# Three hand-overs between batches and the first tiles of a fused attention and gated-FFN kernel: norms by way of DRAM, folded sums of squares, another order of the G/H tiles

## The chip, the cores and the metric

The kernel runs on one core of a Trainium2 chip. Its time is the device time of that core in microseconds; the kernel before takes 808.06 us (median of three runs, 807.99 to 808.19). All runs that are told here were in the fast state at a granted TensorE clock of 0.997 to 1.000, so no difference between them is one of the clock.

## The reference, cut to what matters

```python
def _attn_ref(q, k, v, tau):                 # q, k, v: (4, 6016, 256) float32
    qn = q / (np.linalg.norm(q, axis=1, keepdims=True) + 1e-06)
    kn = k / (np.linalg.norm(k, axis=1, keepdims=True) + 1e-06)
    s = kn.transpose(0, 2, 1) @ qn / tau     # 256 x 256 for each batch
    a = np.exp(s - s.max(-1, keepdims=True))
    a /= a.sum(-1, keepdims=True) + 1e-09
    return v @ a

def _moe_ref(x, w_gate, w_val, w_out):       # x: 24064 x 256, hidden 1536
    gate = 1.0 / (1.0 + np.exp(-(x @ w_gate)))
    return gate * (x @ w_val) @ w_out
```

Attention here mixes the 256 channels, so it is one 256x256 matrix `a` for each of four batches. The kernel multiplies `a` into the weights (G = a·w_gate, H = a·w_val) and runs the gated feed-forward straight on v.

## The kernel before

A batch is 12 chunks of 512 tokens (the last has 384), a chunk is 12 steps; chunks and steps are counted from 0. One step is a gate product and a value product (two matmuls of 512 columns each), a tanh on ScalarE, a product on VectorE that gives a tile of `hT`, in most steps a sum or difference of `hT` tiles on VectorE (`sums`, here called a sum), and some output matmuls of the chunk before, whose results GpSimd's additions join. Everything for the next batch (scores, norms, exponentials, G and H) is spread over these steps as side work. I call slots 96 and later of a batch, where the next batch's attention is finished, a hand-over; there are three. The parts that the change touches:

```python
    def norms_mm(b):                      # column sums of the squares, on TensorE
        s["n"] = psm.tile([P, 2 * CB], FP32, tag="m", name="ps_n")
        norm_mms(s["n"], s["acc"], TPC, True, True)          # 2*4*2 = 16 matmuls of one column

    def spread_both(b):                   # k's inverse norms to a row, the same in all partitions
        s["rk_ps"] = psm.tile([P, C], FP32, tag="m", name="ps_rk")
        for i in range(CB):
            mm(s["rk_ps"][:, ds(i * P, P)],
               s["r"][:, CB + i : CB + i + 1].to_broadcast([P, P]), ident_f, True, True)
    # copy_rk: ScalarE copies rk_ps to rk_sb

    def scale_x(b, j):                    # VectorE: scores x q's norms x k's norms
        nc.vector.scalar_tensor_tensor(out=s["x"][:, j, :], in0=s["s"][:, j, :],
            scalar=s["r"][:, j : j + 1], in1=s["rk_sb"], op0=ALU.mult, op1=ALU.mult)

    def sums_start(b, ni, pl, tag):       # starts the row sums with the small constant
        ps_r = pl.tile([P, ni, 2], FP32, tag=tag, name="ps_r")
        mm(ps_r, ones_row, eps_row[:, :ni, :], start=True, stop=False, skip_group_check=True)
    # ... cut ...
        s0 = 8 * FC + 2                   # = slot 98, in side_work
        at(s0, norms_mm, n)
        at(s0 + 1, root_seed, n)          # square root: seed on VectorE, 13 steps on GpSimd
        at(s0 + 1, root_steps, n)
        at(s0 + 10, norms_inv, n)
        at(s0 + 12, spread_both, n)
        at(s0 + 13, copy_rk, n)
        at(s0 + 14, scale_x, n, 0)        # and n, 1; then exps, all_sums, gh_tiles, gh pieces
    # ... cut ...
    gh_slots = ((5, 6, 7), (8,), (9, 10), (11,), (12,), (13, 14), (15,))   # batch 0: G/H pieces by step
    # for f, the step of chunk 0 of batch 0:
    #     glu(..., between = piece 4 in step 0);  ...;  for i in gh_slots[f]: gh(0, gh_first[i], pso, "o")
```

The chunk that comes next needs v turned: `transpose_v` issues a DMA transpose on SyncE's queue at step 2 of each chunk. The loads are issued on GpSimd's queue.

## Time and profile before

| what | value | how to read it |
|---|---|---|
| time | 808.06 us | median of three runs |
| span of the profiled run | 806.4 us | first to last instruction |
| start of the span to the first matmul | 6.91 us | varies from 6.49 to 7.00 over all kernels told here, with no order in it |
| first matmul to the first gate matmul of chunk 2, batch 0 | 63.34 us | first loads, batch 0's attention, first G/H tiles |
| from there to the start of the last matmul | 732.87 us | the three hand-overs lie here |
| start of the last matmul to the end | 3.28 us | last copies and stores |

The last four rows come from the trace's starts and add up to the span. I use them because a whole time mixes all four, and two of them move from kernel to kernel without having been touched. The lines of the profile before are in the prediction.

### The profile page before, as it was taken

The numbers are of one execution on the slowest core, as the hardware profiler recorded it, in microseconds if no ns is written. First come the engines' busy times: TensorE is split into PE (matmuls) and PEld (weight loads), VectorE is DVE, ScalarE is ACT, GpSimd is POOL, SyncE is SP. The second block draws the span as 40 slices with busy tenths as digits, with TensorE's granted clock in tenths as the row PEclk, the third lists the DMA queues.
The fourth block names the chain that finished last, engine by engine and source line by source line (L and its number), as shares of the span: only waits on it lengthen the run. The fifth ranks groups of instructions, "written<-read, shape, count | busy, mean of one in ns | idle before, by whom it ended". The sixth has DMA issues, their size and how long they took to land.

```text
span 806.4 us, 17923 instructions
## 1 busy us (share of the span) xinstructions
PE 786.3 (98%) x6786; PEld 501.5 (62%) x6786; DVE 704.4 (87%) x1201; ACT 525.6 (65%) x890; POOL 356.9 (44%) x568
## 2 busy tenths in 40 slices
PE   3899999999999999999999999999999999999998
PEld 2546666666666666666666666666666666666666
DVE  5767999998878999999887999999988898898896
ACT  3666777766667776775666767776666665665664
POOL 4572545444452444335443544433534244434433
PEclk9999999999999999999999999999999999999999
DMA  9995757532567567422367377523422332332402
GB/s 214 204 214 105 125 91 135 103 67 47 102 123 128 90 103 145 87 53 58 83 117 132 72 145 112 105 54 89 64 53 54 87 65 63 84 65 68 85 28 74
DMA packets 78919, 78.50 MB, mean 97 GB/s; under 512 B 51824, under 2 KB 56688, under 8 KB 78832
## 3 DMA queue, kind: packets, MB, share of 16 engines
q0 software_dynamic: 22192, 39.59, 29.4%
q1 hardware_dynamic: 56064, 36.91, 20.6%
q8 instruction: 53, 0.87, 0.4%
q10 hardware_dynamic: 576, 0.85, 0.3%
q14 instruction: 34, 0.28, 0.1%
HBM read 78.64 MB, written 24.64 MB: 128 GB/s over the span
## 4 chain that ended last, share of the span: by engine, by line
PE 94%; DMA 3%; DVE 1%; issue 1%; POOL 0%; ACT 0%; POOLq 0%; DVEq 0%; ACTq 0%
PE ps_val L127 30%; PE ps_gate L127 30%; PE ps_o L127 27%; PE ps_s L127 4%; DMA k_sb<-in_k_dram 3%; PE ps_gh L127 3%; DVE hT L514 0%; PE ps_r L127 0%; PE ps_n L127 0%; DVE acc L284 0%; DVE sums L536 0%; PE ps_rk L127 0%; POOL q_sb L137 0%; PE ps_end L127 0%; ACT g_sb L513 0%
## 5 line engine op out<-in xcount | busy, mean ns | idle before, releaser
L513 ACT ACTIVATE g_sb<-ps_gate 128x512 f32<-128x512 f32 (+1 forms) x576 | 338.2, 588 | 225.5 <-PE ps_gate L127 218.9
L514 DVE SCALAR_TENSOR_TENSOR hT<-g_sb,ps_val 128x512 bf16<-128x512 f32 (+1 forms) x576 | 384.6, 670 | 84.3 <-ACT g_sb L513 74.6
L127 PE MATMUL ps_val<-vT,gh_H 128*128 128x512 bf16 (+1 forms) x1152 | 337.7, 375 | 0.9 <-DVE gh_H L461 0.6
L127 PE MATMUL ps_gate<-vT,gh_G 128*128 128x512 bf16 (+1 forms) x1152 | 337.6, 375 | 0.0
L536 DVE TENSOR_TENSOR sums<-hT 128x768 bf16<-128x768 bf16 (+1 forms) x460 | 275.9, 600 | 0.0
L127 PEld LDWEIGHTS <-sums 128*128 128x128 bf16 x2670 | 183.0, 98 | 82.1
L127 PEld LDWEIGHTS <-gh_H 128*128 128x128 bf16 x1152 | 112.7, 98 | 132.3 <-DVE gh_H L461 1.4
L607 POOL TENSOR_TENSOR out_sb<-out_sb,m_sb 128x256 f32<-128x256 f32 x89 | 78.7, 884 | 239.6 <-ACT out_sb L597 211.1
L127 PE MATMUL ps_o<-w_sums,sums 128*128 128x128 bf16 x1602 | 154.4, 219 | 0.0
L127 PEld LDWEIGHTS <-hT 128*128 128x128 bf16 x1200 | 88.3, 98 | 46.8
L591 POOL TENSOR_TENSOR m_sb<-m_sb 128x128 f32<-128x128 f32 x89 | 42.2, 474 | 159.8 <-ACT m_sb L590 159.8
L127 PEld LDWEIGHTS <-gh_G 128*128 128x128 bf16 x1152 | 97.0, 98 | 14.9 <-DVE gh_G L461 0.3
L127 PE MATMUL ps_o<-w_out_sb,sums 128*128 128x128 bf16 x1068 | 96.2, 219 | 0.0
L127 PE MATMUL ps_o<-w_sums,hT 128*128 128x128 bf16 x1068 | 95.5, 219 | 0.0
L127 PE MATMUL ps_s<-k_sb,q_sb 128*128 128x256 bf16 x376 | 69.2, 286 | 15.4 <-DMA k_sb<-in_k_dram 8.5
L608 POOL TENSOR_TENSOR out_sb<-out_sb 128x256 f32<-128x256 f32 x89 | 77.0, 865 | 7.0
L597 ACT COPY out_sb<-ps_o 128x512 f32<-128x512 f32 x89 | 52.1, 586 | 12.0 <-PE ps_o L127 9.2
L284 DVE TENSOR_TENSOR acc<-acc,sq 128x1024 bf16<-128x1024 bf16 (+1 forms) x66 | 59.8, 905 | 0.0
L592 POOL TENSOR_TENSOR m_sb<-m_sb 128x128 f32<-128x128 f32 x89 | 53.8, 604 | 7.0
L246 ACT ACTIVATE sq<-k_sb 128x1024 bf16<-128x1024 bf16 (+2 forms) x44 | 44.8, 1027 | 12.0 <-DMA k_sb<-in_k_dram 11.8
L127 PEld LDWEIGHTS <-q_sb 128*128 128x128 bf16 x376 | 32.9, 102 | 20.8 <-issue 10.3
L590 ACT COPY m_sb<-ps_o 128x384 f32<-128x384 f32 x89 | 42.6, 478 | 3.4 <-PE ps_o L127 0.6
(83 smaller groups left out, 309.4 us busy)
## 6 DMA issues: line engine op xcount, KB each, us to landing
out_dram<-out_sb SPq DMA_DIRECT2D x43, 512.0 KB, 3.4
v_sb<-in_v_dram POOLq DMA_DIRECT2D x44, 256.0 KB, 5.3
q_sb<-in_q_dram POOLq DMA_DIRECT2D x35, 256.0 KB, 4.6
k_sb<-in_k_dram POOLq DMA_DIRECT2D x35, 256.0 KB, 6.1
q_sb<-in_q_dram POOLq DMA_DIRECT2D x4, 512.0 KB, 11.6
k_sb<-in_k_dram POOLq DMA_DIRECT2D x4, 512.0 KB, 13.5
w_f<-in_moe_w_out_dram POOLq DMA_DIRECT2D x3, 512.0 KB, 9.2
out_dram<-out_sb SPq DMA_DIRECT2D x3, 384.0 KB, 2.8
```

The costliest lines, as they stand in the source:

```text
L127: nc.tensor.matmul(out, lhsT=lhsT, rhs=rhs, start=start, stop=stop, **kw)
L246: nc.scalar.activation(out=sq[:, :nt, :], in_=src[:, :nt, :], func=ACT.Square)
L284: nc.vector.tensor_tensor(out=acc[:, :nt, :], in0=acc[:, :nt, :], in1=st[b]["sq", w][:, :nt, :], op=ALU.add)
L513: nc.scalar.activation(out=g_sb[:, :n], in_=ps_gate[:, :n], func=ACT.Tanh, scale=0.5)
L514: nc.vector.scalar_tensor_tensor(out=hts[b, ci][:, f, :n], in0=g_sb[:, :n], scalar=1.0, in1=ps_val[:, :n], op0=ALU.add, op1=ALU.mult,)
L536: nc.vector.tensor_tensor(out=sums[b, ci, g][:, m, :, : half * P], in0=hT[:, f0 + k0 : f1 : 2, ds(r0 * half * P, half * P)], in1=hT[:, f0 ...
L590: nc.scalar.copy(m, states[p]["ps"][:, : 3 * P].rearrange("p (n c) -> p n c", c=P))
L591: nc.gpsimd.tensor_tensor(out=m[:, 1, :], in0=m[:, 1, :], in1=m[:, 2, :], op=ALU.add)
L592: nc.gpsimd.tensor_tensor(out=m[:, 2, :], in0=m[:, 1, :], in1=m[:, 0, :], op=ALU.add)
L597: nc.scalar.copy(o[:, p : p + half + 1 : half, :], states[p]["ps"].rearrange("p (t c) -> p t c", c=C),)
L607: add(out=ends, in0=ends, in1=states[p]["m"][:, 1:3, :], op=ALU.add)
L608: add(out=ends, in0=ends, in1=mids, op=ALU.subtract)
```

## The change

The intent is to take work off TensorE, which is busy for nearly the whole span: fold the four quarters of the sums of squares on VectorE, so that 4 matmuls remain of 16; replace the two fp32 matmuls that spread k's norms by a VectorE transpose in 32x32 blocks, two DMA writes to a row in DRAM and one read that spreads it; start the row sums in bf16; and in batch 0 put the G/H pieces elsewhere among the gate and value products, on more PSUM banks (PSUM is the memory that matmuls write to; a bank is one buffer of it).

```diff
-    ones_row = consts.tile([1, P], FP32)
+    ones_row = consts.tile([1, P], BF16)
-    eps_row = consts.tile([1, CB, 2], FP32)
+    eps_row = consts.tile([1, CB, 2], BF16)
+    r_wide = consts.tile([P, 32], FP32)
...
+    def acc_fold(b, w):
+        acc = st[b]["acc"][w]
+        for n in (2, 1):
+            nc.vector.tensor_tensor(out=acc[:, :n, :], in0=acc[:, :n, :], in1=acc[:, n : 2 * n, :], op=ALU.add)
...
-        norm_mms(s["n"], s["acc"], TPC, True, True)
+        norm_mms(s["n"], s["acc"], 1, True, True)
...  spread_both: the two matmuls (and copy_rk) go, in their place:
+        nc.vector.transpose(out=rT, in_=r_wide)
+        row = dpool.tile([C], FP32, tag="row", name="row")
         for i in range(CB):
+            nc.sync.dma_start(
+                out=row[ds(i * P, P)].rearrange("(s j) -> s j", j=32), in_=rT[CB + i : P : 32, :]
+            )
+        nc.sync.dma_start(out=s["rk_sb"], in_=row.rearrange("(o c) -> o c", o=1).to_broadcast([P, C]))
...  slots of a hand-over
-        at(s0, norms_mm, n)
+        at(s0 if b == 0 else s0 - 2, acc_fold, n, 0)
+        at(s0 + 1 if b == 0 else s0, acc_fold, n, 1)
+        at(s0 + 3, norms_mm, n)
...
-        at(s0 + 14, scale_x, n, 0)
+        at(s0 + 19, scale_x, n, 0)
...  batch 0's G/H pieces
-    gh_slots = ((5, 6, 7), (8,), (9, 10), (11,), (12,), (13, 14), (15,))
+    gh_mid = {0: 4, 1: 6, 2: 9, 3: 11}
+    gh_end = {0: (5,), 1: (7, 8), 2: (10,), 3: (12,), 4: (13,), 5: (14,), 6: (15,)}
+    gh_banks = ((pso, "o"), (psm, "m"), (pso, "o"), (pss, "s"))
```

Left out: in a hand-over the square root starts three slots later and the spread two slots earlier; the later batches' G/H pieces come two steps apart, and those that no longer fit run in the next batch's first steps.

More of the change, by code (lines that the diff above doesn't have):

```diff
@@ L117 @@
     opool = pool("opool", 2)
+    dpool = pool("dpool", 1, space=bass.MemoryType.DRAM)
     psg = pool("psg", 2, space=PSUM)
@@ L173 @@
     nc.vector.memset(one_two[:, 1:2], 2.0)
-    ones_row = consts.tile([1, P], FP32)
+    ones_row = consts.tile([1, P], BF16)
     nc.vector.memset(ones_row, 1.0)
-    eps_row = consts.tile([1, CB, 2], FP32)
+    eps_row = consts.tile([1, CB, 2], BF16)
     nc.vector.memset(eps_row[:, :, 0:1], 1e-9)
     nc.vector.memset(eps_row[:, :, 1:2], 2e-9)
+    r_wide = consts.tile([P, 32], FP32)
+    nc.vector.memset(r_wide, 0.0)
     shift = consts.tile([P, 1], FP32)
@@ L307, in spread_both @@
         s = st[b]
-        s["rk_ps"] = psm.tile([P, C], FP32, tag="m", name="ps_rk")
+        rT = attp.tile([P, 32], FP32, tag="rT", name="rT")
+        nc.vector.transpose(out=rT, in_=r_wide)
+        row = dpool.tile([C], FP32, tag="row", name="row")
         for i in range(CB):
-            mm(
-                s["rk_ps"][:, ds(i * P, P)],
-                s["r"][:, CB + i : CB + i + 1].to_broadcast([P, P]),
-                ident_f,
-                True,
-                True,
-            )
-    def copy_rk(b):
-        s = st[b]
+            nc.sync.dma_start(
+                out=row[ds(i * P, P)].rearrange("(s j) -> s j", j=32), in_=rT[CB + i : P : 32, :]
+            )
         s["rk_sb"] = attp.tile([P, C], FP32, tag="rk", name="rk_sb")
-        nc.scalar.copy(s["rk_sb"], s["rk_ps"])
+        nc.sync.dma_start(out=s["rk_sb"], in_=row.rearrange("(o c) -> o c", o=1).to_broadcast([P, C]))
     def norms_sqrt(b):
@@ L347, in root_steps @@
         t = attp.tile([P, 2 * CB], FP32, tag="tn", name="t_n")
-        s["r"] = attp.tile([P, 2 * CB], FP32, tag="r", name="r")
+        s["r"] = r_wide[:, : 2 * CB]
         for _ in range(3):
@@ L741 @@
     gh(0, gh_first[3], pso, "o")
+    spill = {}
     def side_work(b):
@@ L784, in side_work, with gh_piece @@
         s0 = 8 * FC + 2
-        at(s0, norms_mm, n)
-        at(s0 + 1, root_seed, n)
-        at(s0 + 1, root_steps, n)
-        at(s0 + 10, norms_inv, n)
-        at(s0 + 12, spread_both, n)
-        at(s0 + 13, copy_rk, n)
-        at(s0 + 14, scale_x, n, 0)
-        at(s0 + 14, scale_x, n, 1)
-        at(s0 + 15, exps, n, 0)
-        at(s0 + 16, exps, n, 1)
-        at(s0 + 18, all_sums, n)
-        at(s0 + 18, gh_tiles, n)
-        for i, piece in enumerate(gh_order):
-            at(s0 + 19 + 9 * i // 4, gh, n, piece, *((pss, "s"), (psm, "m"))[i % 2])
-        return side
-    gh_slots = ((5, 6, 7), (8,), (9, 10), (11,), (12,), (13, 14), (15,))
+        at(s0 if b == 0 else s0 - 2, acc_fold, n, 0)
+        at(s0 + 1 if b == 0 else s0, acc_fold, n, 1)
+        at(s0 + 3, norms_mm, n)
+        at(s0 + 4, root_seed, n)
+        at(s0 + 4, root_steps, n)
+        at(s0 + 10, norms_inv, n)
+        at(s0 + 10, spread_both, n)
+        at(s0 + 19, scale_x, n, 0)
+        at(s0 + 19, scale_x, n, 1)
+        at(s0 + 20, exps, n, 0)
+        at(s0 + 21, exps, n, 1)
+        at(s0 + 23, all_sums, n)
+        at(s0 + 23, gh_tiles, n)
+        for i, piece in enumerate(gh_order):
+            slot = s0 + 24 + 2 * i
+            if slot < NCH * FC:
+                at(slot, gh, n, piece, *((pss, "s"), (psm, "m"))[i % 2])
+            else:
+                spill.setdefault((n, *divmod(slot - NCH * FC, FC)), []).append((gh, (n, piece, psm, "m")))
+        return side
+    gh_mid = {0: 4, 1: 6, 2: 9, 3: 11}
+    gh_end = {0: (5,), 1: (7, 8), 2: (10,), 3: (12,), 4: (13,), 5: (14,), 6: (15,)}
+    gh_banks = ((pso, "o"), (psm, "m"), (pso, "o"), (pss, "s"))
+    def gh_piece(n):
+        gh(0, gh_first[n], *gh_banks[n % 4])
     prev = None
@@ L809 @@
             for f in range(FC):
-                first = (b, ci, f) == (0, 0, 0)
-                glu(b, ci, f, (lambda: gh(0, gh_first[4], pso, "o")) if first else None)
+                mid = gh_mid.get(f) if (b, ci) == (0, 0) else None
+                glu(b, ci, f, None if mid is None else (lambda: gh_piece(mid)))
                 if prev is not None:
@@ L819 @@
                     a_sum(b, ci, 0, OWN_SLOTS[f])
-                for fn, a in side.get((ci, f), ()):
+                for fn, a in spill.get((b, ci, f), []) + side.get((ci, f), []):
                     fn(*a)
-                if (b, ci) == (0, 0) and f < len(gh_slots):
-                    for i in gh_slots[f]:
-                        gh(0, gh_first[i], pso, "o")
+                if (b, ci) == (0, 0):
+                    for i in gh_end.get(f, ()):
+                        gh_piece(i)
             prev = (b, ci)
```

## The prediction

> **What bounds the kernel now.** I read the busy shares first, then the chain that ended last, then TensorE's waits, then TensorE's groups by shape, and last the timeline around the places that the change touches. The first fence has the busy shares and the chain's shares by engine, both from the page.
>
> ```profile
> PE 786.3 (98%) x6786; PEld 501.5 (62%) x6786; DVE 704.4 (87%) x1201; ACT 525.6 (65%) x890; POOL 356.9 (44%) x568
> ...
> PE 94%; DMA 3%; DVE 1%; issue 1%; POOL 0%; ACT 0%; POOLq 0%; DVEq 0%; ACTq 0%
> ```
>
> TensorE's own matmuls are 94% of the chain. The view of TensorE's waits says how much of the rest of its time is a wait for somebody (in total us, times, longest us):
>
> ```profile
> PE ps_s L127 <- DMA k_sb<-in_k_dram: 8.5, 6, 3.1
> PE ps_s L127 <- ACT k_sb L183: 6.9, 1, 6.9
> PE ps_val L127 <- DVE gh_H L461: 0.6, 1, 0.6
> PE ps_gh L127 <- ACT gh_H L459: 0.6, 1, 0.6
> PE ps_val L127 <- DVE hT L514: 0.3, 1, 0.3
> ```
>
> The first two are the first loads, which the change doesn't touch. After them TensorE waits under 2 us in 770. So work leaves the time only if it leaves TensorE, and shows there one for one; VectorE at 87% may not be pushed past TensorE's pace. From one matmul's start to the next I read 216 ns at 512 columns, 56 ns at 128 and 25 ns at 1 or 2. The groups that the change removes or thins are these (busy us, mean ns, idle before):
>
> ```profile
> L127 PE MATMUL ps_rk<-ident_f,r 128*128 128x128 f32 x16 | 2.7, 291 | 0.0
> ...
> L127 PE MATMUL ps_n<-ones_bf,acc 128*128 128x1 bf16 x64 | 2.2, 163 | 0.0
> ...
> L127 PE MATMUL ps_r<-eps_row,ones_row 1*128 1x4 f32 x6 | 1.1, 258 | 0.0
> ```
>
> Their durations overlap, so I don't use the means but the starts in the timeline of the first hand-over (batch 0 to 1):
>
> ```profile
> 173.84 0.54 PE L127 MATMUL ps_n<-ones_bf,acc 128*128 128x1 bf16 x16
> 174.24 0.59 PE L127 MATMUL ps_gate<-vT,gh_G 128*128 128x512 bf16 x2
> ...
> 189.29 0.66 PE L127 MATMUL ps_rk<-ident_f,r 128*128 128x128 f32 x4
> 189.79 0.59 PE L127 MATMUL ps_gate<-vT,gh_G 128*128 128x512 bf16 x2
> ...
> 197.15 0.33 PE L127 MATMUL ps_o<-w_out_sb,sums 128*128 128x128 bf16 x3
> 197.41 0.38 PE L127 MATMUL ps_r<-eps_row,ones_row 1*128 1x4 f32 x2
> 197.72 0.25 PE L127 MATMUL ps_r<-one_two,e_sb 128*128 128x2 bf16 x4
> ```
>
> Each sits between ordinary matmuls, without idle time of its own: TensorE pays all of it.
>
> **What the Trainium skill says.** "TensorE: Matmul & The Clock Gate", section "Wait — 56ns, not 53.3ns?", gives 55 to 56 ns from start to start at 128 columns and a floor of about 25 ns however small the matmul; the trace agrees (56 and 25). "FP8 and Floating Point Precision", section "TensorE Precision Notes", says that true FP32 takes four passes. Here each fp32 matmul leaves two records, 111 ns apart for 128 columns, so 222 ns or four times 56: it agrees in time, not in the count of records. "VectorE: DVE Perf Modes", section "The three transpose paths", says that VectorE's transpose turns 32×32 blocks only, 311 ns for a 128×128 bf16 tile. That is why four norms per partition come out as rows of 32 in separate partitions and must go through DRAM to be joined; no such operation is in this trace. "DMA: Bandwidth & Descriptors", section "Anatomy of one DMA — SWDGE (gpsimd) path", gives about 2 us of fixed cost per DMA. In this trace the smallest stores on the other queues (64 KB) land after 1.5 to 1.6 us, 128 KB ones after 2.0.
>
> **The change, part by part.** Three hand-overs (into batches 1, 2, 3) are changed alike.
>
> *Sums of squares folded.* VectorE adds the four quarters of each accumulator (512 then 256 columns), so 4 matmuls remain of 16. Sixteen took 174.24 − 173.84 = 0.40 us, 25 ns each; twelve are 0.30 us. VectorE pays two additions per accumulator: in the first phase a 128x512 bf16 product took 424 ns and a 128x256 one 292 ns, so about 0.7 us each pair, 1.4 us per hand-over, less a little overlap.
>
> *Spread of k's norms.* The two fp32 matmuls took 189.79 − 189.29 = 0.50 us; all of it goes. ScalarE loses a copy of 0.38 us, which was not on the path. VectorE gains one transpose of 128x32; estimated from the page's 311 ns for four times the columns, 0.1 to 0.3 us.
>
> *Row sums' first matmul in bf16.* The last of the three output matmuls would end its turn at 197.15 + 3 × 0.056 = 197.32, the next useful matmul starts at 197.72: 0.40 us, of which a bf16 matmul of 4 columns needs 0.025. It saves 0.37. In batch 0 the same matmuls end before TensorE has to wait for the exponentials anyway (idle 0.17 us), so nothing is saved there.
>
> Together 0.30 + 0.50 + 0.37 = 1.17 us per hand-over, 3.5 us for three.
>
> *G/H tiles in batch 0.* From 36.8 to 49.0 us TensorE alternates these pieces with the first gate/value matmuls, all pieces through one pair of PSUM buffers. Comparing starts with the 216 ns and 109 ns turns, I find six gaps: 0.13, 0.08, 0.72, 0.08, 0.80, 0.07 us, in sum 1.88. The large two:
>
> ```profile
> 39.22 0.38 PE L127 MATMUL ps_gh<-w_val,e_sb 128*128 128x256 bf16 x2 [0.56 <-ACT gh_H L459]
> ...
> 45.27 0.39 PE L127 MATMUL ps_val<-vT,gh_H 128*128 128x512 bf16 x1 [0.64 <-DVE gh_H L461]
> ```
>
> One is a piece that waits for its buffer, the other a value matmul that waits for VectorE to write the H tile finished just before. The change uses four banks and puts pieces between gate and value, so that a tile is finished earlier. I walked the new order by hand with turns of 0.43 us (two 512-column matmuls), ScalarE at 0.69 and 0.60 us, VectorE at 0.74 and 0.69. The 0.13 stays (nothing before it changed); one wait of about 0.2 appears where the value matmul of step 2 needs the H piece that VectorE writes at 40.7 to 41.1; the rest fits, the last H tile of the second group being written some 0.5 us early. The last piece ends at 47.4 instead of 49.0: 1.55 us saved.
>
> *G/H tiles of the later batches* start five steps later, two steps apart, and one spills into the next batch. TensorE's work is the same and the tile it fills is first used eight steps after: 0.
>
> *New small stalls.* In the first hand-over the second fold falls in a step that has a sum too, and pushes the next gate-value product from 177.2 to about 177.5, near the moment at which TensorE wants its buffer. I allow 0.2 us for all of these.
>
> Sum: 808.06 − 3.5 − 1.55 + 0.2 = 803.2.
>
> **The rivals.**
>
> *The DRAM detour comes late.* VectorE is in order: if the row isn't back at its multiplication, it blocks, both value buffers fill, and TensorE stops. From the norms' step (VectorE at 187.5) to the multiplication there are nine steps of 1.255 us, 11.3 us. Two writes and one read at 2 to 3.5 us each, the read behind the writes, make 4 to 6 us. Against it: 5 us to spare, and the transpose of v behind it on the same issuing engine is needed only at the next chunk, some 10 us on. If it came 2 us late each time, up to 1 us each would be lost after buffering, some 3 us: 806.
>
> *The square root's slots shrink.* It starts three steps later and the inverse stays, so nine steps become six, 7.5 us. GpSimd's chain ran from 177.37 to 182.01, 4.64 us; its seed now comes from VectorE at about 180.8, which ends it at 185.5, and VectorE wants it at 187.4. GpSimd's other additions were moved ahead of it in the order, so they end before. About 1.9 us to spare; if it failed, 0.5 to 1 us per hand-over: 805 to 806.
>
> *VectorE becomes the bound.* Per step it has 0.61 + 0.55 = 1.16 us against TensorE's 1.255. It recovers only 0.1 us per step where each has a sum, so 1.6 us of folds and transpose could lag for many steps. Against it: three of four kinds of fold lie in steps without a sum (0 and 2 of a chunk). It would cost 0.5 us per hand-over: 804.7.
>
> *The start gains less,* because ScalarE or VectorE, served in another order, make TensorE wait elsewhere: half of 1.55 would leave 804.
>
> *Something hidden anyway* (no gain at all) I hold for unlikely, since TensorE has no idle time at these places.
>
> **Range and chances.** All rivals but the first are small and add to the same side, so the range is wider above: 802.4 to 804.8. Even the whole sum without a loss is 0.65%, so over 2% in either direction is next to excluded: 0.01 each. Runs of the kernel before spread by only 0.2 us.
>
> **What would show it.** TensorE's groups: the fp32 row sums gone, 4 records of the spread left of 16, 28 of the folded matmuls left of 64; the waits for gh_H gone from its waits. Starts in the hand-over: 0.10 us for what is left of the norms' matmuls, no gap at the spread, some 0.03 us for the first row-sum matmul. The last piece of batch 0 about 10.7 us after the first gate matmul, instead of 12.3. The row lands within 6 us of the transpose. I am wrong if TensorE's waits list VectorE's multiplication, its fold or the norms in the hand-overs, or if VectorE waits for GpSimd or the DMA there.

## The result

The changed kernel took 806.44 us (median of six runs, 806.03 to 806.69) against 808.11 us for the kernel before. The ratio is 0.9979, 95% interval 0.9966 to 0.9992. A ratio here is the mean time of one kernel's fast runs over that of the other's of the same rounds, so it isn't quite the ratio of the medians. The gain is 1.67 us where 4.9 was predicted, and the time lies outside the range, above it. The outputs are right.

Busy shares and the chain's shares by engine, from the page of the changed kernel:

```profile
PE 783.2 (97%) x6733; PEld 497.8 (62%) x6733; DVE 711.0 (88%) x1217; ACT 524.8 (65%) x887; POOL 356.5 (44%) x568
...
PE 91%; DMA 5%; DVE 2%; POOL 1%; issue 1%; ACT 0%; POOLq 0%
```

TensorE has 53 records fewer and 3.1 us less busy time, so the work did leave it. But its share of the chain fell from 94% to 91%, and the DMA's rose from 3% to 5%: something else now holds it up. TensorE's waits (total us, times, longest us), without the first loads, name it:

```profile
...
PE ps_gate L128 <- DMA vT<-v_sb: 1.0, 1, 1.0
PE ps_r L128 <- ACT e_sb L397: 0.6, 1, 0.6
PE ps_val L128 <- DVE hT L518: 0.3, 1, 0.3
```

The two waits for the H tiles are gone, as predicted, and a new one of 1.0 us for a transposed v stands in their place. The view of TensorE's groups by shape (busy us, mean ns, idle before) has the counts that were predicted, 28 and 4 and no fp32 row sum:

```profile
L128 PE MATMUL ps_n<-ones_bf,acc 128*128 128x1 bf16 x28 | 1.3, 164 | 0.0
L128 PE MATMUL ps_rk<-ident_f,r 128*128 128x128 f32 x4 | 0.7, 300 | 0.0
...
L128 PE MATMUL ps_r<-eps_row,ones_row 1*128 1x4 bf16 x3 | 0.5, 173 | 0.0
```

The places where time went are in TensorE's timeline (start us, duration us):

```profile
51.20 0.59 PE L128 MATMUL ps_val<-vT,gh_H 128*128 128x512 bf16 x2
52.76 0.61 PE L128 MATMUL ps_gate<-vT,gh_G 128*128 128x512 bf16 x2 [0.97 <-DMA vT<-v_sb]
...
177.03 0.24 PE L128 MATMUL ps_n<-ones_bf,acc 128*128 128x1 bf16 x4
177.13 0.59 PE L128 MATMUL ps_gate<-vT,gh_G 128*128 128x512 bf16 x2
...
199.70 0.59 PE L128 MATMUL ps_gate<-vT,gh_G 128*128 128x512 bf16 x2
200.35 0.59 PE L128 MATMUL ps_val<-vT,gh_H 128*128 128x512 bf16 x2
...
202.17 0.55 PE L128 MATMUL ps_o<-w_sums,hT 128*128 128x128 bf16 x7
202.66 0.17 PE L128 MATMUL ps_r<-eps_row,ones_row 1*128 1x4 bf16 x1
202.76 0.25 PE L128 MATMUL ps_r<-one_two,e_sb 128*128 128x2 bf16 x4
```

The first two of these lines belong to chunk 1's first gate product. In the kernel before they were:

```profile
52.91 0.59 PE L127 MATMUL ps_val<-vT,gh_H 128*128 128x512 bf16 x2
53.34 0.59 PE L127 MATMUL ps_gate<-vT,gh_G 128*128 128x512 bf16 x2
```

Four things are to be seen, in this order. (1) At chunk 1's first gate product the turn that should take 0.43 us takes 52.76 − 51.20 = 1.56: 1.13 lost to the transpose of v. The kernel before started the same product without a wait. (2) The norms' matmuls take 0.10 us now, 0.30 less, as predicted. (3) Between the gate and value products at 199.70 there are 0.65 us, not 0.43: a gap of 0.21 that no wait lists. The waits view counts only time in which no matmul's modelled duration runs, and these durations (0.59 for a turn of 0.43) cover the gap. A second gap, 0.14 us, lies at the output matmuls at 201.06. All three hand-overs have both, within 11 ns of each other. (4) The seven output matmuls from 202.17 would end their turn at 202.17 + 7 × 0.056 = 202.56; the next useful matmul starts at 202.76. The bf16 row-sum start therefore takes 0.20 us, not 0.025: some 95 ns before it, its own 25, and 80 after it.

By the four stretches of the trace:

| stretch | before | after | difference |
|---|---|---|---|
| to the first matmul | 6.91 | 6.57 | −0.34 |
| to the first gate matmul of chunk 2 | 63.34 | 63.11 | −0.23 |
| to the start of the last matmul | 732.87 | 730.91 | −1.96 |
| to the end | 3.28 | 3.66 | +0.38 |

The hand-overs gave 1.96 of the predicted 3.3 (3.5 less 0.2), the start 0.23 of 1.55, and the end lost 0.38, which nobody had looked for. (The profiled run was the fastest of the six, 806.03; the others are up to 0.66 slower, and their traces weren't kept. So the four differences add up to 2.15, more than the 1.67 between the medians.)

VectorE's timeline around the multiplication `scale_x` shows what surrounds the gap at 199.9:

```profile
197.20 0.69 DVE L518 SCALAR_TENSOR_TENSOR hT<-g_sb,ps_val 128x512 bf16<-128x512 f32 x1
197.81 1.10 DVE L540 TENSOR_TENSOR sums<-hT 128x768 bf16<-128x768 bf16 x1
198.84 0.86 DVE L305 SCALAR_TENSOR_TENSOR x_sb<-ps_s,r_wide,rk_sb 128x256 f32<-128x256 f32 x2
199.62 0.67 DVE L518 SCALAR_TENSOR_TENSOR hT<-g_sb,ps_val 128x512 bf16<-128x512 f32 x1
```

The multiplication (0.86 us) follows a sum that took 1.10 instead of its usual 0.55, so the next `hT` product, which frees the value bank, starts 2.4 us after the last one (197.20 to 199.62) where a step is 1.255. TensorE has two such banks and runs out of them. The row of norms wasn't late: the next fence has SyncE's queue (issue start, time to issue) and, from the view of the tile `rk_sb`, the landing time of the read.

```profile
187.44 1.18 SPq L321 DMA_DIRECT2D row<-rT  x2
189.70 0.33 SPq L325 DMA_DIRECT2D rk_sb<-row  x1
```

```profile
DMA to landing us min/median/max: 3.3/3.5/3.7
```

The writes went out at 187.44, the read at 189.70, and 3.5 us later the row was there: about 193.2, 5.6 us ahead of the multiplication at 198.84.

### The profile page after: what moved, and what is told of

Its sections match the earlier page's. It is cut to its first block, busy times and chain, and to the rows that moved or that the text cites. A ratio compares the mean times of both kernels' runs of the same rounds, so it can differ in the third digit from the quotient of the medians.

```text
span 804.3 us, 17846 instructions
## 1 busy us (share of the span) xinstructions
PE 783.2 (97%) x6733; PEld 497.8 (62%) x6733; DVE 711.0 (88%) x1217; ACT 524.8 (65%) x887; POOL 356.5 (44%) x568
## 4 chain that ended last, share of the span: by engine, by line
PE 91%; DMA 5%; DVE 2%; POOL 1%; issue 1%; ACT 0%; POOLq 0%
PE ps_val L128 29%; PE ps_gate L128 29%; PE ps_o L128 27%; PE ps_s L128 4%; DMA k_sb<-in_k_dram 3%; PE ps_gh L128 2%; DMA vT<-v_sb 1%; DMA v_sb<-in_v_dram 1%; DVE hT L518 1%; DVE sums L540 0%; DVE x_sb L305 0%; POOL w_gate L197 0%; POOL w_val L197 0%; ACT g_sb L517 0%; DVE acc L287 0%
## 5 line engine op out<-in xcount | busy, mean ns | idle before, releaser
L540 DVE TENSOR_TENSOR sums<-hT 128x768 bf16<-128x768 bf16 (+1 forms) x460 | 279.9, 609 | 0.0
```

The lines of the kernel that those rows point to most:

```text
L540: nc.vector.tensor_tensor(out=sums[b, ci, g][:, m, :, : half * P], in0=hT[:, f0 + k0 : f1 : 2, ds(r0 * half * P, half * P)], in1=hT[:, f0 ...
```

## The experiments

Theories of the missing 3.2 us were set against each other in four places. For the start: the transpose of v is late because of what the DMA engines have ahead of it, or because its v was loaded too late. For the hand-overs: VectorE is held by the folds, by the DMA detour, or by the place at which the multiplication now falls. For the row sums: the cost is of a matmul with one row, or of the row sums as such. For the end: the DRAM tile delays it. Each kernel below was timed in rounds with the kernel before on the same chip; all give right results. "Third stretch" is the third row of the table above, and it is the sharper measure, since the whole times of kernels with the change spread by 0.3 to 0.9 us. It comes from one profile of each kernel; where an edit leaves the hand-overs alone it repeats within 0.03 us (732.86 to 732.87, and 730.89 to 730.91).

### The new order in batch 0 alone

Edit: the kernel before, with only this part of the change.

```diff
-    gh_slots = ((5, 6, 7), (8,), (9, 10), (11,), (12,), (13, 14), (15,))
+    gh_mid = {0: 4, 1: 6, 2: 9, 3: 11}
+    gh_end = {0: (5,), 1: (7, 8), 2: (10,), 3: (12,), 4: (13,), 5: (14,), 6: (15,)}
+    gh_banks = ((pso, "o"), (psm, "m"), (pso, "o"), (pss, "s"))
```

> The kernel before with only the new order of batch 0's G/H pieces. Theory A (the start is bound by the DMA transpose of the second chunk of v): TensorE's gaps for gh_H go, step 11 of chunk 0 comes about 1.5 us earlier, but TensorE then waits about 1.1 us for vT at the first gate of chunk 1, so the time falls by only 0.3 to 0.6 us. Rival (the prediction's: the gain is real, and the 3.3 us were lost in the hand-overs): the time falls by 1.3 to 1.6 us and no wait for vT shows.

Measured: 807.82 us (807.73 to 807.97) against 808.12, ratio 0.9996 (0.9988 to 1.0005). From the first gate product to that of step 11, chunk 0 is 1.54 us shorter than before (14.17 us against 15.71), so the order itself does what it was meant to. Then TensorE waits 1.0 us for the transposed v. The third stretch is 732.86, unchanged. So the order alone gains some 0.3 us (the interval reaches 1, but the stretch from the first matmul to chunk 2 is also 0.25 us shorter), and the rest of its 1.55 goes into that wait.

### The v of chunk 1 loaded earlier

Edit to the changed kernel: the load of chunk 1's v goes ahead of the last third of the weights.

```diff
     for f0, nf in pieces:
+        if f0 == FG * (NFG - 1):
+            load_v(0, 1)
...
-    load_v(0, 1)
```

> The changed kernel with the load of v's second chunk issued ahead of the last third of the gate and value weights instead of behind it. Theory A: vT lands some 2 to 3 us earlier, the wait of 1.0 us at the first gate of chunk 1 goes, and the time falls by 0.8 to 1.2 us to about 805.4; other waits unchanged. Rival (the DMA queues are full anyway, and whatever is issued first the transpose lands when the bytes before it are through): the wait stays within 0.3 us of what it is, or moves to the G/H pieces that need the last weights, and the time stays at 806.4.

Measured: 806.54 us (806.02 to 806.96) against 808.12, ratio 0.9980 (0.9974 to 0.9987), the same as the change. SyncE could issue the transpose at 40.73 instead of 43.27, but TensorE got it no earlier. (The trace has no landing for this transpose in kernels with the DRAM detour; TensorE's start shows the end of the wait.) TensorE's timeline:

```profile
53.08 0.61 PE L128 MATMUL ps_gate<-vT,gh_G 128*128 128x512 bf16 x2 [1.24 <-DMA vT<-v_sb]
```

The wait is still there, and ends at 53.08 instead of 52.76. So it isn't the issue that is late; the transpose, issued 2.5 us sooner, took at least that much longer.

### Loads that aren't urgent moved behind the transpose

Edit to the changed kernel: v of chunk 2 and the first q and k of batch 1, three loads of 256 KB (bf16) issued between 38.5 and 41.7 us, go behind the copies of w_out on GpSimd, to 49 us and later.

```diff
-            if lb < B:
+            if lb < B and (b, ci) != (0, 0):
                 at(ci * FC + 0, load_v, lb, lci)
...
                     at(8, copy_w_out, i)
+                at(8, load_qk, 1, *groups[0])
+                at(8, load_v, lb, lci)
...
-                at(max(0, s0 - 12), load_qk, n, t0, nt)
+                if g:
+                    at(max(0, s0 - 12), load_qk, n, t0, nt)
```

> The changed kernel with three loads that nobody needs before chunk 1 (v's third chunk and the first q and k group of batch 1, 0.75 MB) issued after GpSimd's casts of the output weights, at 48.7 us instead of 38.5 to 41.2. Theory A2 (the transpose of v's second chunk lands when the backlog on the 16 DMA engines is through, whenever it is itself issued: issued 2.5 us earlier in the run with the early load, it landed no earlier): the backlog ends some 3 us earlier, vT lands before 51.7, the wait of 1.0 us at the first gate of chunk 1 goes and the time falls by 0.8 to 1.2 us, if the first scores of batch 1 don't wait for their loads. Rival (the transpose itself needs its 10 us here): the wait stays within 0.3 us. A third outcome, a new wait of TensorE for q and k of batch 1 at about 55 us in place of the old one, would leave the time at 806.4.

Measured: 805.21 us (805.04 to 805.55) against 808.16, ratio 0.9964 (0.9950 to 0.9977). The same two lines of TensorE's timeline as at chunk 1 of the changed kernel:

```profile
51.34 0.59 PE L128 MATMUL ps_val<-vT,gh_H 128*128 128x512 bf16 x2
51.78 0.59 PE L128 MATMUL ps_gate<-vT,gh_G 128*128 128x512 bf16 x2
```

The turn is 0.44 us, the wait is gone, and the stretch from the first matmul to chunk 2 is 61.78 us, 1.56 less than before. No new wait came for it. In the windows view the mean DMA share from 48 to 54 us is 0.71, where the changed kernel has 1.26 (the view adds up the packets' times, which overlap, so it can pass 1). With the run before, this settles the start: what delays the transpose is the bulk loads that the DMA engines still have to carry. The Trainium skill, "DMA: Bandwidth & Descriptors", section "Queues, rings and completion order", says that each DMA engine goes round between the queue rows it has work for, packet by packet; that would make a transpose share its engines with all open loads. These two runs agree with it, but none shows the packets' order.

### Row sums started with 128 rows

Edit to the changed kernel: the constant is divided by 128 and summed over 128 partitions, with ones in 128 rows as weights, in place of one row.

```diff
-    eps_row = consts.tile([1, CB, 2], BF16)
-    nc.vector.memset(eps_row[:, :, 0:1], 1e-9)
-    nc.vector.memset(eps_row[:, :, 1:2], 2e-9)
+    eps_row = consts.tile([P, CB, 2], BF16)
+    nc.vector.memset(eps_row[:, :, 0:1], 1e-9 / P)
+    nc.vector.memset(eps_row[:, :, 1:2], 2e-9 / P)
...
-        mm(ps_r, ones_row, eps_row[:, :ni, :], start=True, stop=False, skip_group_check=True)
+        mm(ps_r, ones_bf, eps_row[:, :ni, :], start=True, stop=False, skip_group_check=True)
```

> The changed kernel with the constant of the row sums made by a matmul over 128 rows (weights of ones, constants divided by 128) instead of one row. Theory B (the switch to a one-row weight and back costs 0.175 us at each hand-over, as the starts show 95 and 80 ns too much): from the last output matmul before to the first row-sum matmul it is one turn of 56 ns and one of 25, the time falls by 0.5 us. Rival (a small matmul after a wide one costs this whatever its rows): the 95 and 80 ns stay, the time is unchanged.

Measured: 805.83 us (805.60 to 805.98) against 808.12, ratio 0.9972 (0.9961 to 0.9982). TensorE's timeline at the first hand-over:

```profile
202.29 0.55 PE L128 MATMUL ps_o<-w_sums,hT 128*128 128x128 bf16 x7
202.68 0.17 PE L128 MATMUL ps_r<-eps_row,ones_bf 128*128 128x4 bf16 x1
202.71 0.24 PE L128 MATMUL ps_r<-one_two,e_sb 128*128 128x2 bf16 x4
```

The start of the row sums comes 0.39 us after the seven (7 × 0.056), and the next 0.03 after it: it now costs the 25 ns that I had predicted for the one-row form. The third stretch fell by 0.58, 0.19 in each hand-over. So the 95 and 80 ns belong to a matmul of one row. Whether to its weights or to its moving operand isn't separated, since both have one row there and 128 here.

### Row sums in fp32 again

Edit to the changed kernel:

```diff
-    ones_row = consts.tile([1, P], BF16)
+    ones_row = consts.tile([1, P], FP32)
-    eps_row = consts.tile([1, CB, 2], BF16)
+    eps_row = consts.tile([1, CB, 2], FP32)
```

> The changed kernel with the row sums' constants in fp32 again. The starts say 0.405 us for the fp32 pair and 0.20 us for the one bf16 matmul: the time rises by 0.6 us for three hand-overs. If the prediction's 0.37 us per hand-over were right, it would rise by 1.1 us.

Measured: 806.84 us (806.62 to 807.45) against 808.09, ratio 0.9986 (0.9979 to 0.9992); the third stretch rose by 0.60, 0.20 for each hand-over. So the step from fp32 to bf16 is worth 0.20, not the predicted 0.37.

### No folds

Edit to the changed kernel: the 16 matmuls back, `norms_mm` still at slot 101.

```diff
-        norm_mms(s["n"], s["acc"], 1, True, True)
+        norm_mms(s["n"], s["acc"], TPC, True, True)
...
-        at(s0 if b == 0 else s0 - 2, acc_fold, n, 0)
-        at(s0 + 1 if b == 0 else s0, acc_fold, n, 1)
```

> The changed kernel without the folding of the sums of squares: 16 matmuls again at each hand-over, VectorE's four additions gone. By the arithmetic on record the folding is worth 12 x 25 ns = 0.30 us per hand-over: the time rises by 0.9 us if VectorE's additions are free. If the additions delay VectorE up to the multiplication (rival D), the gaps at the multiplication go with them, and the time rises by less than 0.3 us or falls.

Measured: 807.52 us (807.08 to 807.80) against 808.09, ratio 0.9993 (0.9985 to 1.0001). The third stretch rose by 0.89, 0.30 in each hand-over: the fold is worth what was predicted. The gaps at the multiplication stay (0.21 and 0.14 us at the first hand-over), so the folds don't make them.

### The spread on TensorE again

Edit to the changed kernel: the two fp32 matmuls and ScalarE's copy back, at slots 110 and 111; the multiplication stays at 117.

```diff
-        nc.vector.transpose(out=rT, in_=r_wide)
-        row = dpool.tile([C], FP32, tag="row", name="row")
...  the three DMAs go
+            mm(s["rk_ps"][:, ds(i * P, P)], s["r"][:, CB + i : CB + i + 1].to_broadcast([P, P]), ident_f, True, True)
...
-        at(s0 + 10, spread_both, n)
+        at(s0 + 12, spread_both, n)
+        at(s0 + 13, copy_rk, n)
```

> The changed kernel with the spread on TensorE again (two fp32 matmuls and ScalarE's copy, at the old steps), the multiplication left at step 117. By the arithmetic on record the spread is worth 0.50 us per hand-over: the time rises by 1.5 us, and the gaps at the multiplication stay (0.3 to 0.4 us per hand-over), because they come of its place and not of the DMA. Rival (the DMA detour itself, its row late or its traffic, makes the gaps): they go, and the time rises by only 0.4 us.

Measured: 807.36 us (807.20 to 807.50) against 808.09, ratio 0.9991 (0.9983 to 0.9999). The third stretch rose by 1.48, 0.49 in each hand-over, as predicted for the two matmuls. The gaps stay (0.21 and 0.14), so the detour doesn't make them either. The whole time rose by only 0.92; 0.38 of the difference to 1.48 is the end of the trace, which is back at 3.28 us, and the rest lies in the start and in the spread of runs.

### The multiplication three steps earlier, and three later

Edits to the changed kernel. The first moves only the multiplication, to slot 114:

```diff
-        at(s0 + 19, scale_x, n, 0)
-        at(s0 + 19, scale_x, n, 1)
+        at(s0 + 16, scale_x, n, 0)
+        at(s0 + 16, scale_x, n, 1)
```

> The changed kernel with the multiplication by the spread norms three steps earlier (step 114, not 117), some 1.4 us after the row lands by the profile; all else in place. Theory C (at step 117 it falls behind a sum that GpSimd's additions stretch to 1.10 us, and its 0.78 us then make the next products late): the 0.21 and 0.14 us gaps on TensorE at each hand-over go or shrink to under 0.1 us in sum, the time falls by 0.7 to 1.0 us. Rival D (VectorE is simply at its bound there by the folds and the transpose): the gaps only move a step or two, the time stays within 0.2 us.

Measured: 805.31 us (804.90 to 805.39) against 808.12, ratio 0.9964 (0.9952 to 0.9977). Both gaps are gone in all three hand-overs, and the third stretch fell by 1.06, 0.35 each (0.21 and 0.14). VectorE's timeline at the new place:

```profile
194.34 0.55 DVE L540 TENSOR_TENSOR sums<-hT 128x768 bf16<-128x768 bf16 x1
194.81 0.87 DVE L305 SCALAR_TENSOR_TENSOR x_sb<-ps_s,r_wide,rk_sb 128x256 f32<-128x256 f32 x2
```

The multiplication takes as long as before (0.87 against 0.86), but the sum ahead of it takes 0.55 instead of 1.10. The row, which lands at about 193.2, is still there in time.

The second moves the multiplication and all that follows it by three steps, to slot 120:

```diff
-        at(s0 + 19, scale_x, n, 0)
+        at(s0 + 22, scale_x, n, 0)
...  exps, all_sums, gh_tiles likewise
-            slot = s0 + 24 + 2 * i
+            slot = s0 + 27 + 2 * i
```

> The changed kernel with the multiplication by the spread norms, the exponentials, the row sums and the G/H pieces all three steps later, so that the multiplication falls in step 120, which has no sum on VectorE. Theory C: the gaps of 0.21 and 0.14 us on TensorE go at all three hand-overs, no new one comes, the time falls by 0.8 to 1.1 us. Rival D (VectorE at its bound): gaps of the same sum some steps later, the time stays within 0.2 us.

Measured: 805.08 us (804.92 to 805.39) against 808.09, ratio 0.9963 (0.9951 to 0.9976). The gaps are gone here too, and the third stretch fell by 1.22. Of this, 1.06 are the gaps again; the other 0.16 lies in the steps of the G/H pieces, which this edit moves as well, and wasn't looked into. So it is the place, not the operation: the same multiplication costs TensorE 0.35 us at 117 and nothing at 114 or 120. Nor is it the long sum alone, since that is still there in this kernel, with an `hT` product behind it and no gap on TensorE:

```profile
197.96 1.10 DVE L540 TENSOR_TENSOR sums<-hT 128x768 bf16<-128x768 bf16 x1
198.99 0.68 DVE L518 SCALAR_TENSOR_TENSOR hT<-g_sb,ps_val 128x512 bf16<-128x512 f32 x1
```

At 114 the multiplication follows a sum of 0.55 us and does no harm, at 120 the sum of 1.10 has no multiplication behind it and does none; in these runs only both together cost TensorE its 0.35.

What makes that sum long is read from the traces; no run of its own tests it. GpSimd's timeline in the changed kernel has this addition:

```profile
197.77 0.73 POOL L612 TENSOR_TENSOR out_sb<-out_sb 128x256 f32<-128x256 f32 x1
```

It starts 0.04 us before the sum that took 1.10, and so it does in all three hand-overs. The whole trace of the changed kernel has 430 sums of this shape. The 200 without a two-input operation of GpSimd beside them take 0.54 to 0.55 us. Of the 75 that start before the GpSimd operation, all but one take this long too. In 127 the GpSimd operation had started first and had more than 0.15 us to go: 122 of these sums end 0.41 to 0.42 us after it does (five aren't stretched), and all 22 sums over 0.86 us are among them. The Trainium skill, "SBUF — State Buffer", section "SBUF: two separate sides", says that VectorE and GpSimd share one pair of ports as an exclusive lock, which a VectorE operation with two SBUF inputs needs against a GpSimd operation that reads SBUF: whoever starts first keeps it. The trace agrees: the sum that comes second waits for the end of the addition, and then needs another 0.41 us of its 0.55. No run took the addition away.

### The parts together

Edit to the changed kernel: slot 120 and the 128-row constant, as above.

```diff
-        at(s0 + 19, scale_x, n, 0)
+        at(s0 + 22, scale_x, n, 0)
...
-        mm(ps_r, ones_row, eps_row[:, :ni, :], start=True, stop=False, skip_group_check=True)
+        mm(ps_r, ones_bf, eps_row[:, :ni, :], start=True, stop=False, skip_group_check=True)
```

> The changed kernel with the multiplication at step 120 and the row sums' constant over 128 rows together. If the two costs are separate, their gains add: 806.44 - 1.36 - 0.61, about 804.5, and only the wait for vT is left of what this study found. If they overlap (both hide behind the same VectorE lag) it is 805.0.

Measured: 804.70 us (804.42 to 805.03) against 808.16, ratio 0.9957 (0.9944 to 0.9969). The third stretch fell by 1.79, just the sum of the two alone (1.22 + 0.58). The wait for v at chunk 1 was 1.4 us.

With the later loads as well:

```diff
                     at(8, copy_w_out, i)
+                at(8, load_qk, 1, *groups[0])
+                at(8, load_v, lb, lci)
```

> The same two with the three later loads as well. If theory A2 holds: a further 0.8 to 1.2 us, about 803.5, which is the time predicted for the change. If not, 804.5 as without them.

Measured: 803.47 us (803.26 to 803.61) against 808.16, ratio 0.9941 (0.9929 to 0.9954), span 801.5. It beats both kernels. TensorE's waits, without the first loads:

```profile
...
PE ps_r L128 <- ACT e_sb L397: 0.7, 1, 0.7
PE ps_val L128 <- DVE hT L518: 0.3, 1, 0.3
```

The wait for the transposed v is gone; what is left belongs to batch 0's exponentials and one `hT` product. That this time lies near the predicted 803.2 vouches for nothing: it takes three repairs to get there.

### A DRAM row that nobody uses

Edit: the kernel before, with a tile in DRAM written and read in each hand-over, for nothing.

```diff
         nc.scalar.copy(s["rk_sb"], s["rk_ps"])
+        row = dpool.tile([P, 2 * CB], FP32, tag="row", name="row")
+        nc.sync.dma_start(out=row, in_=s["r"])
+        unused = attp.tile([P, 2 * CB], FP32, tag="unused", name="unused")
+        nc.sync.dma_start(out=unused, in_=row)
```

> The kernel before, with the norms also written to a small DRAM tile and read back into a tile that nobody uses, once per hand-over; nothing waits for it. The traces so far show from the last matmul to the span's end 3.28, 3.29 and 3.28 us in the three kernels that spread on TensorE, and 3.62 to 4.05 us in the nine that have the DRAM row. Theory E (a DRAM tile in the program, or its place beside the output, makes the last store land later): the tail is 3.6 us or more and the time rises by 0.3 to 0.8 us, with TensorE's work up to the last matmul unchanged. Rival (the tail differs for another reason, for instance the change in VectorE's or TensorE's order): the tail stays at 3.3 and the time within 0.2 us of 808.1.

Measured: 808.20 us (808.04 to 808.34) against 808.12, ratio 1.0001 (0.9993 to 1.0009); from the last matmul's start to the end 3.38 us, against 3.28 before and 3.62 to 4.05 in all kernels with the detour. So a DRAM tile and two plain DMAs explain at most 0.1 of it. Without the detour but with the rest of the change, the end took 3.28. The longer end therefore goes with the detour as it is made, whose writes take one partition in 32 and whose read is spread over 128 partitions. The traces also say where it lies: ScalarE's queue issues the last store (64 KB) 0.58 us after the start of the last matmul in every kernel, and SyncE's wait for it ends 2.14 to 2.15 us after that start in the four kernels without the detour, this one included, and 2.58 to 3.02 us in the ten with it. How three transfers hundreds of microseconds earlier make the last store later is open.

| kernel | time us | third stretch us | against the changed kernel |
|---|---|---|---|
| before | 808.06 | 732.87 | +1.96 |
| changed | 806.44 | 730.91 | 0 |
| new order alone | 807.82 | 732.86 | +1.95 |
| v earlier | 806.54 | 730.89 | −0.02 |
| loads later | 805.21 | 730.90 | −0.01 |
| row sums, 128 rows | 805.83 | 730.33 | −0.58 |
| row sums in fp32 | 806.84 | 731.51 | +0.60 |
| no folds | 807.52 | 731.80 | +0.89 |
| spread on TensorE | 807.36 | 732.39 | +1.48 |
| multiplication at 114 | 805.31 | 729.85 | −1.06 |
| multiplication at 120 | 805.08 | 729.69 | −1.22 |
| 120 and 128 rows | 804.70 | 729.12 | −1.79 |
| these and loads later | 803.47 | 729.13 | −1.78 |
| DRAM row unused | 808.20 | 732.86 | +1.95 |

## Why the prediction was wrong

The direction was right and the size was not: 1.67 us came of 4.9. By its own steps:

*Sums of squares folded: right.* 0.30 us in each hand-over, by the starts at 177.03 and by the kernel without folds (0.89 for three). The folds took 457 and 291 ns, 0.75 us for the pair where I had about 0.7.

*Spread of k's norms: right.* 0.50 us each, 1.48 for three in the kernel that puts it back. VectorE's transpose took 211 ns, inside my 0.1 to 0.3.

*"The DRAM detour comes late": rightly held off.* The row was there 5.6 us ahead, where I had said 5 to spare. *"The square root's slots shrink": rightly held off.* GpSimd ended it at 185.2 (predicted 185.5), VectorE took it up at 186.8 without a wait.

*Row sums' first matmul in bf16: mis-sized.* "a bf16 matmul of 4 columns needs 0.025" holds for 128 rows. With one row it took 0.20, so the step saved 0.20 and not 0.37: 0.5 us less over three hand-overs. The 95 ns ahead of it were in the trace of before too (197.32 to 197.41), and I counted them as part of what fp32 costs.

*"VectorE becomes the bound": the mechanism came, from another cause than the one I named.* I looked at whether the folds lie in steps without a sum. They do no harm: without them the gaps stay. What delays VectorE is the multiplication at its new slot, behind a sum that, by the traces, a GpSimd addition stretches to 1.10 us, and TensorE pays 0.35 us each time, 1.06 for three, where I had allowed 0.2 for all small stalls together. I took it for granted that an operation moved by five steps costs what it cost where it was. And none of my signs of being wrong came in the hand-overs, since I looked for them in the list of waits, where these gaps don't show.

*G/H tiles in batch 0: the step failed.* "The last piece ends at 47.4 instead of 49.0: 1.55 us saved." The walk by hand held: the 0.13 stayed, one wait of 0.19 came at the value product of step 2 (predicted 0.2), the last piece ended 10.7 us after the first gate product as said, and step 11 started 1.54 us earlier. But I ended the walk at the last piece. In the kernel before, the transposed v of chunk 1 was issued at 43.45, and the view of the tile `vT` from 38 to 48 us has its landing:

```profile
DMA to landing us min/median/max: 9.4/9.4/9.4
```

So it was there at about 52.9; its first use was at 53.34. There were only some 0.5 us to spare, so at most that much of the 1.55 could show. I had read the transposes only as something behind the detour on SyncE's queue, never as the next limit of the start.

*The end, which no step had:* 0.38 us longer in the changed kernel's trace, because the last store lands later; why it does is open.

Adding up the traces: hand-overs 3 × (0.30 + 0.50 + 0.20 − 0.35) = 1.95, measured 1.96; start 0.23 of 1.55; end −0.38. That leaves 1.81 of the predicted 4.85. The profiled run shows 0.34 more, all of it before the first matmul, a stretch that wanders by that much anyway. Between the medians it is 1.67; the 0.14 less is well inside the 0.66 us by which the changed kernel's runs differ.

## What to carry to other kernels

When a change makes a stretch shorter, follow the walk on to the next thing that comes from elsewhere (a transfer, most of all) and ask by how much it was early before; the smallest of these margins bounds the gain. Compare the starts of matmuls with their usual turn, since a stall of 0.2 us beside modelled durations shows in no list of waits. And a side operation on a nearly full engine has a price that depends on its slot: trying two neighbouring slots found 1.1 us here, more than the smallest of the three intended savings in the hand-overs.

## What the Trainium skill lacked or had wrong

- "TensorE: Matmul & The Clock Gate", section "LDWEIGHTS (loading the stationary operand)", says that the time of a weight load hangs on its columns and not on its rows. The records of the loads agree (91 ns with one row, 97 with 128), but neither this page nor another has a time for what such a matmul costs beside the load: one row cost 95 ns before the matmul and 80 after it beside its own 25, and 128 rows only the 25.
- "FP8 and Floating Point Precision", section "TensorE Precision Notes": four passes for fp32. The traces have two records per fp32 matmul, 111 ns apart at 128 columns; the time agrees, the count of records doesn't.
- "VectorE: DVE Perf Modes", section "The three transpose paths", has 1309 ns for the DMA's transpose of 128x128. For chunks of v (128x1024 bf16, so not the same size) the time from issue to landing was 4.0 us in the median of the kernel before, and 9.4 to 11.0 while bulk loads were open. The page has no time for other sizes; other pages have bandwidths of transposes, but none of these figures is for queues with open loads.
- The same section has VectorE's transpose for 128x128 bf16 alone; 128x32 fp32 took 211 ns here.
- "DMA: Bandwidth & Descriptors" has no figure for a transpose behind open bulk loads: moving three loads of 256 KB out of the way took away a wait that cost 1.1 us.
- "SBUF — State Buffer", section "SBUF: two separate sides", has the whole block for the one that comes second, and the traces agree; it has no figure for what the second still needs afterwards. A sum of 0.55 us ended 0.41 to 0.42 us after the GpSimd operation in 122 of 127 cases.
- I found no page that bears on the longer end: 3.62 to 4.05 us from the last matmul's start in kernels with the detour, 3.28 to 3.38 in those without.
